# A pre-LN transformer block of 2048 tokens on one core: stored task places on all engines, a 64-row paired output projection, and transposes of two tiles at once

## The chip, the core and the metric

The kernel runs on one core of a Trainium2 chip. A core has TensorE (PE in the profile, with its weight loads as PEld), VectorE (DVE), ScalarE (ACT), GpSimd (POOL), and SyncE (SP), which here only issues DMAs. Each engine works through its own instruction queue in order and waits on semaphores. The metric is the device time of one execution in microseconds (us); lower is better.

## What is computed

x has 2048 rows of 448 in bf16, 16 heads of 28. The block is layer norm, linear attention with a Hedgehog feature map, a residual, layer norm, a gated unit of width 1792, a residual:

```
qkv = layernorm(x) @ wqkv                      # q, k, v of 16 heads x 28
pq, pk = q @ w_phi[h], k @ w_phi[h]
phi_q = concat(softmax(pq), softmax(-pq))      # phi_k likewise
kv = phi_k^T v ;  z = sum over tokens of phi_k # per head, over the whole sequence
o  = (phi_q kv) / (phi_q . z + 1e-6)
h  = x + o @ wo
g, u = layernorm(h) @ w_gate, layernorm(h) @ w_up
out = h + (sigmoid(g) * u) @ w_down
```

The sum over tokens in `kv` is a barrier: no token's `o` can begin before the last token's keys and values are in.

## The kernel before

The sequence is cut into 16 tiles of 128 rows. The program is a graph of tasks. Each task has an engine, a duration and a latency that the author wrote down, dependences, and where needed PSUM banks. `_Graph.order` lays the tasks out by a list scheduler, in Python, before anything runs: of the tasks that are ready it takes the one that can start first, and among those of an engine that could start within 0.05 us of each other the one with the largest rank. The rank is the length of the modelled work below the task, or a hand-set `bias`. What comes out is a fixed order per engine and a bank for each task; `emit` writes that order out with the semaphore waits. On the chip the order doesn't change, whatever the real durations are.

The stages, in the order in which a token passes them, by task name:

- `bst`, `agg`, `ve` (DVE), `rstd` (POOL, L449), `nm` (DVE, L452), `xn` (ACT, L461; DVE for the first two tiles): the first layer norm, in batches of 1, 1, 2, 4, 4 and 4 tiles. `xT` transposes the normed tile: by PE and an ACT copy (`xTp`, L469, L473) for four tiles, by a DMA transpose from SP (L477) of 128x512 for the other twelve.
- `wT`, `wTe`, `wM`, `W2` (L409 to L432) fold `w_phi` into the key and the query weights. `w_phi` is loaded by four DMAs of 6 KB straight into a zeroed block-diagonal tile. ACT empties all banks of the query fold and half of those of the key fold.
- `kp`, `vp` (PE, L484, L492), `ekp`, `ekm` (two exponentials, ACT), `v1` (ACT copy, L502), `ss`, `rs` (DVE), `phi` (POOL, L510), `kv` (PE, L519) for each tile.
- `q` (PE, L537) in 4 chunks of 512 tokens by 4 head groups, each followed by two exponentials on ACT (L547). `sigld` (L562) loads the sigmoid table on ACT, after all 32 of them.
- `kvz` (DVE) masks the finished `kv`; then per tile `num` (PE, L574, 8 matmuls of 120 columns, each into contiguous PSUM), `ocp` (ACT, L580), and on DVE `rSm`, `rr`, `b`, `c`, `rd`, `o`. `oT` transposes `o` (PE for 2 tiles, a DMA of 128x512 for 14, L620), `wo_` is the output projection of one tile (PE, L628, 4 matmuls of 112 rows), `h` the residual (DVE, L633).
- The second layer norm (`bst2` to `hn`, L664), its transpose `hT` (PE for 2 tiles, DMA for 14, L668), and the gated unit in chunks of 2, 4, 4, 4, 2 tiles: `gu` (L705, L707: 7 pairs of 64-row matmuls, the gate in array rows 0 to 63, the up projection in rows 64 to 127), `sig` (ACT, L714), `hh` (DVE, L722), `dn` (PE, L731, L741), `fin` (DVE, L747), `st` (SP, L749).

`f_warm` (L319) issues matmuls on the identity into a bank that the next PE task will own, where the plan sees PE idle.

```
order():  c = max((c for c in cands if c[0] <= emin + 0.05), key=lambda c: (c[1].rank, -c[1].idx))
wo_:      for g in range(G):
              r = e.matmul(bank[b][:, 0:D], lhsT=oT[:GP, t % 2, g, :], rhs=wo_sb[:, g, :],
                           start=(g == 0), stop=(g == G - 1))
num:      r = e.matmul(bank[bs[sg]][:, g * HL * E:(g + 1) * HL * E], ...
```

Of the kernel before, what the change touches and what calls it, by code (L numbers as in the profile page):

```python
# [5 lines left out]
dt = mybir.dt  # L6
# [4 lines left out]
P = 128  # L11
# [15 lines left out]

class _Task:
    __slots__ = ("name", "eng", "dur", "lat", "fn", "deps", "rank", "kind", "banks", "until", "got",
                 "start", "finish", "idx", "bias", "need", "lock", "hold", "warm")  # L30


class _Graph:
# [3 lines left out]
    PORT2 = ("xn", "rr", "b", "c", "o", "hn", "kvze")  # L37
    LAT = {"pe": 0.22, "act": 0.16, "dve": 0.08, "pool": 0.12, "sp": 0.0}
# [7 lines left out]
    def task(self, name, eng, dur, fn, deps=(), lat=None, bias=0.0, banks=None, until=(), kind=None):  # L46
# [4 lines left out]
        t.lat = self.LAT[eng] if lat is None else lat  # L51
# [4 lines left out]
        t.idx = len(self.tasks)  # L56
        t.need, t.hold, t.warm = list(t.deps), [], 0
# [9 lines left out]
    def order(self):  # L67
        tasks = self.tasks
        children = {n: [] for n in tasks}
# [16 lines left out]
        for n in reversed(topo):  # L86
            t = tasks[n]
            below = max((tasks[c].rank for c in children[n]), default=0.0)
            t.rank = max(below + t.dur + t.lat, t.bias)
# [4 lines left out]
        free = {e: 0.0 for e in self.ENGINES}  # L94
        bank_until = {}
# [19 lines left out]
        while True:  # L115
            best = None
            for e in self.ENGINES:
                cands = []
                for t in ready[e]:
                    est = max(free[e], port) if t.lock else free[e]  # L120
                    for d in t.deps:
                        est = max(est, tasks[d].finish)
                    pick = None
                    if t.banks is not None:
# [6 lines left out]
                        est = max(est, pick[0])  # L131
# [4 lines left out]
                c = max((c for c in cands if c[0] <= emin + 0.05), key=lambda c: (c[1].rank, -c[1].idx))  # L136
# [7 lines left out]
            t.finish = est + t.dur + t.lat  # L144
            if t.lock:
                port = est + t.dur
            if pick is not None:
                t.got = pick[1]
                for b in pick[1]:
                    t.hold += bank_until.get(b, [])  # L150
                    bank_until[b] = list(t.until)
# [9 lines left out]
        end = 0.0  # L161
        for t in done:
            if t.eng == "pe":
                if t.banks is not None and t.got is not None:
                    free_at = max([end] + [tasks[u].finish for u in t.hold] + [self.warm_from])
                    t.warm = max(0, int((t.start - free_at - 0.2) / 0.32))
                end = t.start + t.dur
        return done

    def emit(self, rings):  # L170
# [4 lines left out]
        with ExitStack() as es:  # L175
# [14 lines left out]
            for t in done:  # L190
                for ds in (t.hold, t.need):
# [5 lines left out]
                    if ds is t.hold and t.warm:  # L197
# [3 lines left out]
                        queues["pe"].append(lambda e, t=t: self.warm_fn(e, t.got[0], t.warm))  # L201
# [27 lines left out]
def build(nc, A_x, A_wqkv, A_w_phi, A_wo, B_w_gate, B_w_up, B_w_down, out):  # L229
# [15 lines left out]
    wo_v = A_wo.rearrange("(g hl d) n -> hl d g n", g=G, hl=HL)  # L245
    wd_v = B_w_down.rearrange("(ft p) n -> p ft n", p=P)

    NXD = 2
    NPE = 4
    NPT = 2  # L250
    NXP, NEK, NPHI, NV, NOP, NB2, NSG = 3, 3, 2, 3, 4, 2, 3

    with ExitStack() as es:
# [17 lines left out]
        xn_pad = sb("xn_pad", [P, NXP, KT, P])  # L271
        xnT = sb("xnT", [P, KT, S])
        wqkv_sb = sb("wqkv_sb", [GP, KT, 3 * D])
        Wq2 = sb("Wq2", [GP, KT, D])
        Wk2 = sb("Wk2", [GP, KT, D])
        Wphi = sb("Wphi", [GP, G, GP])
        wo_sb = sb("wo_sb", [GP, G, D])
# [9 lines left out]
        opm = sb("opm", [P, 2, 2, 2, G, E, HL])  # L287
        rSm = sb("rSm", [P, 2, 2 * G, HL], dt.float32)
        rr = sb("rr", [P, 2, 2 * G, HL])
        rden = sb("rden", [P, 2, 2 * G, HL])  # L290
        o_pad = sb("o_pad", [P, 2, 2 * G, P])
        oT = sb("oT", [P, 2, G, P])
# [22 lines left out]
        K = _Graph(nc)  # L315

# [3 lines left out]
        K.warm_fn, K.warm_deps, K.warm_from = f_warm, ["ident"], 1.2  # L320
# [8 lines left out]
        def TS(t):  # L329
            return slice(t * P, (t + 1) * P)  # L330


        task("z_phi", "pool", 0.45, lambda e: e.memset(Wphi[:], 0.0))
        task("ident0", "pool", 0.2, lambda e: e.memset(ident[:], 0.0))
        task("ident", "pool", 0.3, lambda e: e.affine_select(
            out=ident[:], in_=ident[:], compare_op=ALU.not_equal, fill=1.0, base=0, pattern=[[-1, P]],
            channel_multiplier=1), ["ident0"])
        task("z_xn", "pool", 0.3, lambda e: e.memset(xn_pad[:, :, :, GP:P], 0.0))
        task("neghalf", "pool", 0.1, lambda e: e.memset(neghalf[:], -0.5))
        task("v1one", "pool", 0.4, lambda e: e.memset(v1[:, :, :, DH:EV], 1.0))  # L340
# [7 lines left out]

# [9 lines left out]
        task("z_o", "pool", 0.3, lambda e: e.memset(o_pad[:, :, :, GP:P], 0.0))  # L358


        LD = 2.2

        def load(name, dst, src, eng="sp", deps=(), lat=LD, bias=0.0):
            task(name, eng, 0.5, lambda e: e.dma_start(dst, src), deps, lat=lat, kind="in", bias=bias)
# [3 lines left out]
        def load_x(t0, t1, **kw):  # L368
            load(("x", t0), x_sb[:, t0:t1, :], x_t[:, t0:t1, :], **kw)
            for t in range(t0, t1):  # L370
                x_ld[t] = ("x", t0)

        BIG = 1000.0
        load("wk", wqkv_sb[:, :, D:2 * D], wqkv_v[:, :, D:2 * D], bias=BIG, lat=3.4)
        load_x(0, 2, bias=BIG - 1, lat=3.8)
        load_x(2, 4, bias=BIG - 2, lat=4.2)
        load("wv", wqkv_sb[:, :, 2 * D:3 * D], wqkv_v[:, :, 2 * D:3 * D], bias=BIG - 3, lat=5.0)
        load_x(4, 8, bias=BIG - 4, lat=5.4)
# [413 lines left out]
```

## Time and profile before

| what | value |
|---|---|
| time, median of three runs | 233.93 us (233.16 to 235.45) |
| time of the profiled execution | 232.46 us |
| its span, first to last instruction | 230.7 us |
| mean granted TensorE clock | 0.993 |
| busy: PE, DVE, ACT, POOL | 212.6, 133.6, 120.8, 50.8 us |
| chain that ended last, by engine | PE 71%, ACT 11%, DVE 6%, DMA 6%, issue 3% |

Busy time is the union of the recorded instructions of an engine. Matmuls overlap in the pipeline and are recorded with their latency, so a PE that counts as busy can still be issuing at less than its rate; the distance from one start to the next says what a matmul costs in a stream. "Issue" in the chain is time in which an engine waited for nothing that the profile shows. The windows view gives the busy time of each engine in a chosen stretch.

### The profile page before, as it was taken

The page shows a single profiled execution, that of the slowest core. Times are in us where ns is not written, and L with a number is a line of the kernel's source. Part 1 is how long each engine was busy: PE and PEld are TensorE (multiplying, and loading weights), DVE is VectorE, ACT ScalarE, POOL GpSimd, SP SyncE. Part 2 cuts the span into 40 slices and gives each one's busy share as a digit, 9 for nine tenths or more (in the row PEclk, how much of TensorE's full clock was granted, in tenths as well). Part 3 has the DMA queues.
Part 4 walks back from the last instruction along what each step waited for, and adds up shares of the span by engine and source line. Part 5 has one row for each costly group of instructions (what it writes and reads, how often), then busy time and mean ns, then how long its engine had stood idle before and what let it go on. Part 6 is the DMA issues. An engine that isn't in the chain of part 4 may idle for free.

```text
span 230.7 us, 4738 instructions
## 1 busy us (share of the span) xinstructions
PE 212.6 (92%) x1845; PEld 115.3 (50%) x1845; DVE 133.6 (58%) x293; ACT 120.8 (52%) x213; POOL 50.8 (22%) x82
## 2 busy tenths in 40 slices
PE   6577979799989989899999999999999999999994
PEld 3343555466655656544444443444444444588542
DVE  1868889662389978778336666363366464245222
ACT  2498888878999767464424615342353322135000
POOL 4153579667000223041101020010000010100000
PEclk9997999999999999999999999999999999999999
DMA  6912555773543044723610223202002003210011
GB/s 186 295 50 66 139 134 142 159 195 77 146 133 48 0 88 64 117 54 64 126 39 3 40 25 83 60 3 60 20 3 45 3 1 80 67 35 3 21 40 40
DMA packets 37014, 17.04 MB, mean 74 GB/s; under 512 B 28416, under 2 KB 36096, under 8 KB 36992
## 3 DMA queue, kind: packets, MB, share of 16 engines
q1 hardware_dynamic: 36488, 16.72, 31.2%
q8 instruction: 14, 0.23, 0.4%
q10 hardware_dynamic: 504, 0.03, 0.2%
q14 instruction: 8, 0.07, 0.1%
HBM read 8.28 MB, written 1.84 MB: 44 GB/s over the span
## 4 chain that ended last, share of the span: by engine, by line
PE 71%; ACT 11%; DVE 6%; DMA 6%; issue 3%; POOL 1%; ACTq 0%; POOLq 0%; DVEq 0%
PE bank L705 34%; PE bank L731 17%; PE bank L628 4%; PE bank L484 4%; PE bank L537 3%; ACT opm L580 3%; ACT eq L547 3%; DMA Wphi<-in_A_w_phi_dram 2%; PE bank L492 2%; PE bank L519 2%; PE bank L741 2%; DMA oT<-o_pad 2%; ACT xn_pad L461 2%; DVE nm L452 1%; DMA xnT<-xn_pad 1%
## 5 line engine op out<-in xcount | busy, mean ns | idle before, releaser
L705 PE MATMUL bank<-hnT,wgu_sb 64*128 64x512 bf16 (+1 forms) x490 | 89.4, 334 | 1.3 <-DVE rs L638 0.8
L707 PE MATMUL bank<-hnT,wgu_sb 64*128 64x512 bf16 (+1 forms) x490 | 89.5, 334 | 0.0
L714 ACT ACTIVATE sg_sb<-bank 128x512 bf16<-128x512 f32 (+1 forms) x70 | 35.8, 511 | 65.1 <-PE bank L707 63.7
L705 PEld LDWEIGHTS bank<-hnT,wgu_sb 64*128 64x128 bf16 x490 | 44.0, 94 | 41.8 <-ACT sg_sb L714 4.2
L722 DVE TENSOR_TENSOR hh<-sg_sb,bank 128x512 bf16<-128x512 bf16 (+1 forms) x70 | 40.6, 580 | 41.1 <-ACT sg_sb L714 40.8
L707 PEld LDWEIGHTS bank<-hnT,wgu_sb 64*128 64x128 bf16 x490 | 44.0, 94 | 0.0
L731 PE MATMUL bank<-wd_sb,hh 128*128 128x448 bf16 x196 | 39.0, 353 | 0.2 <-DVE x_sb L747 0.2
L640 POOL TENSOR_TENSOR rs<-rs,neghalf 128x1 f32<-128x1 f32 x16 | 9.8, 610 | 122.3 <-DVE rs L638 122.3
L510 POOL TENSOR_TENSOR phi<-ek,rsum 128x896 bf16<-128x896 bf16 x16 | 27.0, 1697 | 12.4 <-DVE rsum L508 4.8
L731 PEld LDWEIGHTS bank<-wd_sb,hh 128*128 128x128 bf16 x196 | 18.4, 98 | 20.3 <-issue 2.3
L747 DVE TENSOR_TENSOR x_sb<-bank,x_sb 128x448 bf16<-128x448 f32 x16 | 10.0, 625 | 25.4 <-PE bank L731 21.6
L505 DVE TENSOR_REDUCE ssum<-ek 128x32 f32<-128x896 bf16 x16 | 17.1, 1076 | 9.3 <-ACT ek L499 9.2
L664 ACT ACTIVATE hn_pad<-x_sb,nm,rs 128x896 bf16<-128x896 bf16 x14 | 15.8, 1129 | 11.5 <-POOL nm L662 11.5
L547 ACT ACTIVATE eq<-bank 112x512 bf16<-112x512 f32 x32 | 17.1, 633 | 2.1 <-PE bank L537 1.9
L492 PE MATMUL bank<-wqkv_sb,xnT 112*128 112x448 bf16 x64 | 14.7, 357 | 2.8 <-ACT v L502 2.8
L484 PE MATMUL bank<-Wk,xnT 112*128 112x448 bf16 x64 | 15.9, 380 | 0.7 <-DMA xnT<-xn_pad 0.7
L537 PE MATMUL bank<-xnT,Wq 112*112 112x512 bf16 x64 | 15.6, 381 | 0.9 <-ACT eq L547 0.9
L580 ACT CAST opm<-bank 128x960 bf16<-128x960 f32 x16 | 15.5, 984 | 0.9 <-PE bank L574 0.9
L628 PE MATMUL bank<-wo_sb,oT 112*128 112x448 bf16 x64 | 14.8, 354 | 1.0 <-DMA oT<-o_pad 0.9
L444 DVE BATCH_NORM_STATS2 st<-x_sb 128x6 f32<-128x448 bf16 x16 | 9.3, 609 | 5.2 <-DMA x_sb<-in_A_x_dram 5.2
L461 ACT ACTIVATE xn_pad<-x_sb,nm,rs 128x448 bf16<-128x448 bf16 x14 | 10.1, 767 | 2.7 <-DVE nm L452 2.7
L633 DVE TENSOR_TENSOR x_sb<-bank,x_sb 128x448 bf16<-128x448 f32 x16 | 9.9, 622 | 2.1 <-PE bank L628 1.8
(75 smaller groups left out, 200.8 us busy)
## 6 DMA issues: line engine op xcount, KB each, us to landing
out_dram<-x_sb SPq DMA_DIRECT2D x16, 112.0 KB, 1.7
wgu_sb<-in_B_w_gate_dram SPq DMA_DIRECT2D x7, 224.0 KB, 3.8
wgu_sb<-in_B_w_up_dram SPq DMA_DIRECT2D x7, 224.0 KB, 4.1
wd_sb<-in_B_w_down_dram SPq DMA_DIRECT2D x7, 224.0 KB, 4.1
x_sb<-in_A_x_dram SPq DMA_DIRECT2D x3, 448.0 KB, 8.4
wqkv_sb<-in_A_wqkv_dram SPq DMA_DIRECT2D x3, 392.0 KB, 5.8
x_sb<-in_A_x_dram SPq DMA_DIRECT2D x2, 224.0 KB, 4.1
wo_sb<-in_A_wo_dram SPq DMA_DIRECT2D x4, 98.0 KB
```

What stands on the lines that cost most here:

```text
L484: r = e.matmul(bank[b][:, 0:D], lhsT=xnT[:GP, kt, TS(t)], rhs=Wk2[:, kt, :], start=(kt == 0), stop=(kt == KT - 1))
L492: r = e.matmul(bank[b][:, 0:D], lhsT=xnT[:GP, kt, TS(t)], rhs=wqkv_sb[:, kt, 2 * D:3 * D], start=(kt == 0), stop=(kt == KT - 1))
L510: task(("phi", t), "pool", 1.72, lambda e, t=t, s=s: e.tensor_tensor(phi[:, t % NPHI, :, :].rearrange("p a (h d) -> p (a h) d", d=DH), ek[ ...
L537: r = e.matmul(bank[b][:GP, :], lhsT=Wq2[:, kt, g * GP:(g + 1) * GP], rhs=xnT[:GP, kt, c * 512:(c + 1) * 512], start=(kt == 0), stop=(kt = ...
L547: task((key, g, c), "act", 0.5, lambda e, g=g, c=c, sg=sg, nm=nm: e.activation(eq[c][:, sg, g, :], bank[got(nm)[0]][:GP, :], ACT.Exp, scal ...
L580: task(("ocp", t), "act", 0.88, lambda e, t=t: e.copy(opm[:, (t // 2) % 2, :, t % 2, :, :, :].rearrange("p b g e h -> p b (g e h)"), pair[ ...
L628: r = e.matmul(bank[b][:, 0:D], lhsT=oT[:GP, t % 2, g, :], rhs=wo_sb[:, g, :], start=(g == 0), stop=(g == G - 1))
L705: e.matmul(bank[bg][:, 0:N], lhsT=wgu_sb[0:64, j, fs], rhs=hnT[0:64, j, cs], start=(j == 0), stop=(j == NJ - 1))
L707: r = e.matmul(bank[bu][:, 0:N], lhsT=wgu_sb[64:P, j, fs], rhs=hnT[64:P, j, cs], start=(j == 0), stop=(j == NJ - 1), tile_position=(64, 0))
L714: task(("sig", f_, c), "act", 0.5 if n == 4 else 0.3, lambda e, j=j, N=N, nm=nm: e.activation(sg_sb[:, j % NSG, 0:N], bank[got(nm)[0]][:, ...
L722: task(("hh", f_, c), "dve", 0.68 if n == 4 else 0.42, lambda e, j=j, N=N, nm=nm, f_=f_, c=c: e.tensor_tensor(hhT[c % 2][:, f_, 0:N], sg_s ...
L731: r = e.matmul(bank[b][:, 0:D], lhsT=hhT[c % 2][:, f_, ts], rhs=wd_sb[:, f_, :], start=(f_ == 0), stop=(f_ == FT - 1))
```

## The change

- **Order.** Every task gets a place from a table, `PLACE`, of some 950 whole numbers, by task kind in the order of creation; the rank of a task is minus its place. `order` still takes the earliest start first; the place decides among tasks of one engine within 0.05 us. The modelled durations are replaced (for instance `gu` 1.55 to 1.511, `hh` 0.68 to 0.605, `h` 0.62 to 0.545), hops between engines, a change between 64-row and full-row matmuls (`SWITCH` 0.098) and a DMA rate are added to the model.
- **Warm matmuls** now go into any bank that is free for the time (`plan_warm`), up to 110 us of the plan, instead of only into the bank of the waiting task.
- **Output projection.** `wo_sb` is laid out as 7 slices of 64 rows, held twice (partitions 0 to 63 and 64 to 127; 8 loads of 100 KB instead of 4). One `wo_` task takes two tiles: 7 pairs of 64-row matmuls, the first tile's in array rows 0 to 63 into one bank, the second's in rows 64 to 127 into another.
- **Transposes.** `xT` by DMA and `oT` by DMA take two tiles at once (7 and 7 instead of 12 and 14). PE transposes only 2 tiles of x instead of 4, and the first two tiles of `o` in one go. One small DMA transpose (`trw`) of the identity is added early.
- **num and o.** `num` writes its 120 columns as 30 runs of 4 fp32 at a stride of 16, so that heads lie innermost; `o` becomes one DVE instruction per tile.
- **Moves between engines.** Half of the query fold's copies and the `v1` copy of 4 tiles go from ACT to DVE; `nm` goes from DVE to POOL with its negation (`ng`) done ahead on DVE; `w_phi` comes by one DMA and is spread by a POOL multiply with the mask (`Wphi`).
- **Loads and batches.** x of tile 0 is loaded first; the loads of x beyond tile 1 come after `wq`. Layer-norm batches are 1, 1 and then 2 tiles. The query fold may use four banks.
- **Tail.** `dnp`, `fin` and `st` of the last two tiles are cut into column halves, `dn` may use two more banks.

```diff
+PLACE = {
+    "mask0": """-51""",
...
+    "q": """-58 -184 399 536 98 -50 14 144 172 167 -1593 -1608 -1566 -332 240 -2""",
...
+}
     def order(self):
...
+        for n, t in tasks.items():
+            if t.prio is not None:
+                t.rank = t.prio
...
+                    if e == "pe" and t.rows64 != rows64:
+                        est += self.SWITCH
                     for d in t.deps:
-                        est = max(est, tasks[d].finish)
+                        x = tasks[d]
+                        est = max(est, x.finish + self.HOP[e] if x.eng != e or e != "pe" else x.finish - 0.17)
...
+    def plan_warm(self, done):
+
+        held = {}
         for t in done:
...
+        end = self.warm_from
+        for t in done:
+            if t.eng != "pe":
+                continue
+            n = int((t.start - end - 0.3) / 0.32)
+            if n > 0 and t.start <= self.warm_to:
+                for b in range(7, -1, -1):
+                    past = [h for h in held.get(b, ()) if h[0] < t.start]
+                    if all(h[1] <= end for h in past):
+                        t.warm, t.warm_bank = n, b
+                        t.hold = list(past[-1][2]) if past else []
+                        break
+            end = max(end, t.start + t.dur)
...
-    NXD = 2
-    NPE = 4
+    XN_DVE = (0, 1)
+    NPE = 2
     NPT = 2
+    QLATE = 3
+    Q_FOLD, Q_EARLY = ("act", "dve"), True
+    XT_ENG = ("act",)
+    V_DVE = (3, 7, 11, 15)
+    BATCHES = [(0, 1), (1, 2), (2, 4), (4, 6), (6, 8), (8, 10), (10, 12), (12, 14), (14, 16)]
...
+        load("wphi", Wphi0[:], A_w_phi.rearrange("(g hl) i j -> (hl i) g j", hl=HL), 25, bias=BIG, eng="act")
+        task("Wphi", "pool", 1.0, lambda e: e.tensor_tensor(
+            Wphi[:].rearrange("p g (h d) -> p g h d", h=HL), Wphi0[:][:, :, None, :].to_broadcast([GP, G, HL, DH]),
+            maskK[:][:, None, :, None].to_broadcast([GP, G, HL, DH]), ALU.mult), ["wphi", "maskK"])
+        task("trw", "sp", 1.25, lambda e: e.dma_start_transpose(out=oT[:, 0, 0, :], in_=ident[:]), ["ident"],
+             lat=2.8, kind="tr")
...
-                task(("nm", a), "dve", 0.17, lambda e, a=a, z=z: e.scalar_tensor_tensor(
-                    nm1[:, a:z], mv1[:, a:z, 0], -1.0, rs1[:, a:z], op0=ALU.mult, op1=ALU.mult), [("rstd", a)])
+                task(("ng", a), "dve", 0.08, lambda e, a=a, z=z: e.tensor_scalar(
+                    nm1[:, a:z], mv1[:, a:z, 0], -1.0, None, op0=ALU.mult), [("agg", t) for t in range(a, z)])
+                task(("nm", a), "pool", 0.2, lambda e, a=a, z=z: e.tensor_tensor(
+                    nm1[:, a:z], nm1[:, a:z], rs1[:, a:z], ALU.mult), [("ng", a), ("rstd", a)])
...
+            elif t % 2 == 0:
+                task(("xT", t), "sp", 1.25, lambda e, t=t: e.dma_start_transpose(
+                    out=xnT[:, t // 2, :, :, :].rearrange("p a k s -> p (a k) s"),
+                    in_=xn_pad[:, (t // 2) % NXP, :, :, :].rearrange("p a k s -> p (a k s)")),
+                    [("xn", t), ("xn", t + 1)], lat=1.78, kind="tr")
...
-                        r = e.matmul(bank[bs[sg]][:, g * HL * E:(g + 1) * HL * E],
+                        r = e.matmul(bank[bs[sg]][:, 0:E * H].rearrange("p (e h) -> p e h", h=H)[:, :, g * HL:(g + 1) * HL],
                                      lhsT=eq[c][:, sg, g, (t % 4) * P:(t % 4 + 1) * P], rhs=kvz[:, sg, g, :, :],
                                      start=True, stop=True)
...
+                for j in range(NJ):
+                    e.matmul(bank[b[0]][:, 0:D], lhsT=oT[0:64, tb, j, :], rhs=wo_sb[0:64, j, :],
+                             start=(j == 0), stop=(j == NJ - 1))
+                    r = e.matmul(bank[b[1]][:, 0:D], lhsT=oT[64:P, tb, j, :], rhs=wo_sb[64:P, j, :],
+                                 start=(j == 0), stop=(j == NJ - 1), tile_position=(64, 0))
...
+            task(("wo_", t), "pe", 1.33, f, [("oT", t)] + [("wo", a, d) for a in range(2) for d in range(4)],
+                 banks=WO_BANKS, until=[("h", t), ("h", t + 1)], rows64=True)
```

## The prediction

> **What bounds the kernel now.** I read the page's slices and chain first: PE 71% of the chain, but 92% busy, which by itself would leave 18 us. So I cut the span into stages at the places where the PE timeline changes character and asked the windows view for each engine's busy time there. Columns: stage, its length, then busy us (and instructions) of PE, PEld, DVE, ACT, POOL, the granted clock, the DMA share, GB/s.
>
> ```profile
> core 0: us, PE busy (x) PEld busy (x) DVE busy (x) ACT busy (x) POOL busy (x), PEclk, DMA share, GB/s
> 0.00:8.45 8.45, 5.58 (x29) 2.85 (x29) 3.29 (x11) 2.25 (x3) 3.58 (x18) 1.00 0.82 221
> 8.45:20.00 11.55, 7.11 (x73) 5.08 (x74) 8.74 (x26) 9.39 (x19) 4.45 (x5) 0.99 0.43 117
> 20.00:50.00 30.00, 26.46 (x204) 16.15 (x203) 23.07 (x43) 25.74 (x53) 19.81 (x14) 0.95 0.58 139
> 50.00:59.90 9.90, 9.90 (x74) 6.44 (x73) 3.89 (x7) 7.92 (x16) 6.50 (x4) 1.00 0.39 96
> 59.90:79.35 19.45, 17.99 (x163) 10.99 (x162) 14.91 (x44) 18.27 (x31) 2.09 (x5) 1.00 0.38 97
> 79.35:98.70 19.35, 16.91 (x236) 11.85 (x238) 15.61 (x44) 12.61 (x23) 3.73 (x9) 1.00 0.50 83
> 98.70:218.90 120.20, 120.20 (x1035) 58.12 (x1032) 61.55 (x122) 44.61 (x71) 10.66 (x30) 1.00 0.18 40
> ```
>
> The kernel is two kernels. From 98.70, where the second `gu` chunk starts, PE never lacks work until the tail. Before that ACT is the fullest engine: 61.3 of the 70.9 us from 8.45 to 79.35, the start of the first `gu`; what PE does there comes late because ACT, or a latency in front of ACT, is late. The waits of ACT between 8 and 80 us (who waited, for whom, total, times, longest) and three steps of the chain (start, length, what) say which:
>
> ```profile
> ACT xn_pad L461 <- DVE nm L452: 2.7, 2, 1.6
> ACT Wk L432 <- PE bank L424: 2.3, 1, 2.3
> ACT v L502 <- PE bank L492: 2.0, 2, 1.2
> ACT eq L547 <- PE bank L537: 1.9, 2, 1.2
> ```
>
> ```profile
> 26.13 1.01 issue
> 27.14 1.02 POOL rs L449
> 28.19 1.66 DVE nm L452
> ```
>
> The largest is the layer-norm batch of four: after the POOL power, `nm`, which takes 0.16 us at other times, lasts 1.65 us while POOL runs `phi` beside it, twice, and ACT stands.
>
> How much PE loses I get from the PE timeline by start-to-start distances, not by busy time: a `kp` or `vp` 0.755 us, a `q` 0.865, a `kv` or `num` 0.42, a `wo_` 0.76, a half-size `gu` 0.765, a fold group of four 0.22. The work done before 98.70 is then 16 x 2 x 0.755 + 16 x 0.865 + 16 x 0.42 + 12 x 0.42 + 8 x 0.76 + 14 x 0.765 + 16 x 0.22 + 2.5 for the other transposes = 72.5 us. PE's first useful matmul starts at 4.95. So 93.75 - 72.5 = 21 us of PE are unused before 98.70, 1.2 of them at changes of row mode, whose price these rows of the timeline show (start, length, instruction):
>
> ```profile
> 121.06 0.38 PE L707 MATMUL bank<-hnT,wgu_sb 64*128 64x512 bf16 x1
> 121.27 0.38 PE L705 MATMUL bank<-hnT,wgu_sb 64*128 64x512 bf16 x1
> 121.27 0.38 PE L707 MATMUL bank<-hnT,wgu_sb 64*128 64x512 bf16 x1
> 121.58 0.93 PE L628 MATMUL bank<-wo_sb,oT 112*128 112x448 bf16 x4
> 122.44 0.39 PE L705 MATMUL bank<-hnT,wgu_sb 64*128 64x512 bf16 x1
> ```
>
> A pair of 512 columns takes 0.215, so the `wo_` could have started at 121.485 and started 0.10 later; four matmuls take 0.76, and the next pair came 0.10 later still. Each change costs 0.10.
>
> **The change part by part**, against the profiled execution: 232.46 us, span 230.7, so 1.8 around it. The median of the runs is 1.5 above that execution.
>
> *The front, up to the first `gu` (79.35).* The bound is ACT. It idles 70.9 - 61.3 = 9.6 us there. The change takes from it four fold copies (0.43 from start to start in the ACT timeline), four `v1` (0.42) and two `xT` copies (0.49): 1.7 + 1.7 + 1.0 = 4.4 us. If ACT were packed the stage would end 14.0 us earlier. The edits that aim at the idle time: batches of two instead of four and `nm` on POOL (nearest row: POOL's 0.19 us product of mean and rstd in the second layer norm, L660) remove both 1.65 us waits and shorten what precedes them; a query fold done early makes `q` available as PE work, and `eq` as ACT work, in the gaps where neither has anything now (its last copy ends at 48.6, first `q` at 51.6). What keeps it below 14: kv sums remain a barrier, POOL still has 16 x 1.70 = 27.2 us of `phi` plus some 7 us, and each tile must pass ACT, DVE, POOL and PE in turn. Ends: 0 (all idle time reappears elsewhere) to 14.0. I take 70%, 9.8 us, because PE and DVE allow it: PE's work to that point is 72.5 - 10.7 - 4.3 = 57.5 us in 64.6, DVE's 54 in 64 of the new length, with some 5 us of `v1` and fold copies added and 3.6 us of `nm` taken away.
>
> *`Wphi`, load order, `trw`.* The first fold matmul waits for the last of four small loads, 5.5 us after issue, at 8.45. One load instead, plus a POOL multiply of 448 columns: the nearest row, `phi` with 896 columns, is 1.70, so 0.85 to 1.7. Against it the one load stands where the first of the four is issued, 1.29 against 2.78, 1.5 us sooner. Net -0.7 to +1.7, I take +0.5. `trw` (1.2 us of SP, as the other transposes) stands in SP's empty stretch from 6 to 17.8 us: nothing is queued behind it that is due. If SP has x loads behind it, it costs those 1.2 us, covered by DVE's backlog of statistics. x of tile 0 in front of `wk` is 112 KB at about 290 GB/s, 0.4 us later for the key transposes, hidden behind the `Wphi` wait.
>
> *From first `gu` to PE saturation (19.35 us).* Useful work is 10.7 + 4 x 0.76 + 3 x 0.42 = 15.0, so 4.3 are lost, 1.2 to mode changes, the rest to waits for `rstd`, `oT` (0.9) and `opm`. `wo_` in 64-row form next to `gu` costs no change. Two tiles per transposition: the 128x896 transposes land after 2.9 us against 2.5 for 128x512, so a pair costs 0.4 more latency for its first tile and 2.1 less than two in a row. Ends 0 to 3.5; I take 1.5.
>
> *PE work in the saturated part.* A pair of 448 columns, scaled from the 0.215 row, takes 0.189; seven are 1.32 us for two tiles against 1.51. Four such pairs fall after 98.70: 0.8. Five of the eight `wo_` there now stand between two `gu`: ten changes at 0.10, 1.0. Together 1.8 (0.8 if they come to stand beside `dn`, where they add changes). A pair holds two banks until both `h` are done instead of one; `gu` has three bank pairs of its own, and `h` is 0.54 from start to start, so nobody waits. `o` as two DVE instructions of 448 columns costs 2 x 0.29 against 0.54 (DVE timeline), 7 x 0.04, beside 60 us of free DVE time.
>
> *`num` into strided PSUM.* No row of this trace has a matmul with a gapped destination. The floor is the present 0.42 per tile. From above, the recorded latency of one such matmul, 0.217, unpipelined: 128 x (0.217 - 0.053) = +21 us of PE. I take 0, since each run of 4 fp32 is written whole and the same 120 values leave; the top end is a rival. The Trainium skill speaks against this edit: "PSUM — Partial Sum Buffer", section Specifications (TRN2), gives cache lines of 8 bytes and says "any non-contiguous AP slows matmuls significantly", without a factor. No row here shows it. Were the factor two, the sum below would be 6.7 us worse, an estimate from that sentence.
>
> *Tail.* The last `fin` is 0.62 and its store 1.7; halves make that 0.31 and a little less: 0.5. Beyond it the same 5.3 us of `dn` per two tiles remain.
>
> Sum: -9.8 + 0.5 - 1.5 - 1.8 - 0.5 = -13.1. 232.46 - 13.1 = 219.4; against the median, 220.8. I say 220.
>
> **The rivals.**
>
> 1. *The gaps close further.* Front 14.0, all 3.5 of the next stage, the rest as above: 232.46 - 14.0 - 3.5 - 1.8 - 0.5 = 212.7, 214 on the median. For it: none of PE, DVE, POOL is full in the front. Against: ACT would have no wait in 57 us.
>
> 2. *The order does little.* The places choose only among tasks within 0.05 us; the order stays greedy, and waits move rather than go. Then only moved work and content count: 2 us of the front, 1.8, 0.5, less 0.5: 228.7, 230 on the median. For it: ACT's waits of 8.45 to 79.35 are many and small (the largest group is 2.7 us). Against: `nm` and the late query fold are causes with a name, and both go.
>
> 3. *Slower: `num` pays for its stride.* At the top price, +21 us of PE: 219.4 + 21 = 240.4, 242 on the median. It decides from 128 x 0.102 us, that is when a `num` matmul takes 0.155 instead of 0.053. For it: nothing in this profile is like it. Against: the same 16-byte pieces per partition, and half of the `num` (those before `gu`) may hide behind ACT.
>
> 4. *An engine gets stuck behind a wait*, as an in-order queue with a fixed order can when a transposition or load lands late: 227 to 234.
>
> **How the numbers follow.** Chances: forecast (216 to 226) 0.58, rival 1 (209 to 216) 0.17, rival 2 (226 to 233) 0.14, rival 3 0.06, rival 4 or another loss 0.05. Leaving out the far ends of rivals 1 and 2 and rival 3, 212 to 229 holds 8 in 10. 1% is 2.3 us, about what a measurement here can tell from no change: faster than 231.6 are the first two and most of rival 2, 0.87; within, 0.05; slower 0.08.
>
> **What would show it.** First `gu` near 70 us instead of 79.35 and second chunk near 88; ACT over 90% busy between 9 and 70; no `nm` row over 0.3 us; `wo_` pairs at 0.19 from start to start, with no 0.10 around them beside `gu`; `num` still 0.42 per tile. It is wrong if ACT's idle time before the first `gu` stays near 9 us, if `num` stretches, or if PE waits appear after the second chunk.

## The result and the profile after

| | before | after |
|---|---|---|
| time, median | 234.33 us (233.16 to 235.45, 4 runs) | 220.74 us (220.06 to 221.35, 4 runs) |
| profiled execution | 232.46 us, span 230.7 | 221.35 us, span 219.6 |
| PE busy in the span | 212.6 us | 206.8 us |
| first `gu` starts | 79.35 us | 75.63 us |
| recorded end of the last matmul | 227.65 us | 216.37 us |

The kernel became faster: ratio 0.942 of the time before, 95% interval 0.9364 to 0.9476. The profiled pair differs by 11.1 us, less than the medians (13.6), since the profiled execution of before was below its median and that of after above it. The sums below go by the profiled pair. Runs over 1.5% above the fastest of their kernel count as slow and are left out of the ratios but not of the medians: two of the four of experiment 3, and of experiment 5 the one that was profiled.

The windows view of the changed kernel, cut where the stages change (stage, length, busy us and instructions of PE, PEld, DVE, ACT, POOL, granted clock, DMA share, GB/s):

```profile
core 0: us, PE busy (x) PEld busy (x) DVE busy (x) ACT busy (x) POOL busy (x), PEclk, DMA share, GB/s
0.00:5.77 5.77, 3.60 (x8) 1.04 (x8) 1.58 (x6) 1.28 (x1) 2.96 (x15) 1.00 0.63 179
5.77:20.00 14.23, 12.53 (x106) 8.81 (x107) 11.91 (x37) 11.67 (x23) 3.74 (x8) 0.88 0.78 178
20.00:50.00 30.00, 26.71 (x200) 15.97 (x199) 23.24 (x48) 26.19 (x55) 25.14 (x21) 1.00 1.06 181
50.00:58.50 8.50, 8.50 (x72) 5.50 (x70) 4.73 (x8) 5.86 (x12) 5.05 (x3) 1.00 0.01 2
58.50:75.60 17.10, 15.32 (x168) 9.31 (x166) 15.02 (x45) 15.70 (x25) 1.49 (x2) 1.00 0.48 122
75.60:100.40 24.80, 24.20 (x317) 17.17 (x317) 23.16 (x71) 15.71 (x25) 8.88 (x24) 1.00 0.38 72
100.40:216.40 116.00, 115.97 (x1052) 61.50 (x1050) 53.36 (x103) 40.04 (x66) 5.27 (x18) 1.00 0.19 38
```

Look at the row 20.00:50.00. PE does 26.71 us of it, hardly more than before (26.46), though ACT, POOL and DVE are not full either, and the DMA share has risen from 0.58 to 1.06. In the next row, which takes in the last `kv` (it ends at 56.65, counted here and below as the start of its last matmul plus 0.05), PE is full: the transpositions are all in by then.

What PE waits for up to 110 us (line, for whom, total, times, longest), and two pieces of the chain of waits between 20 and 60:

```profile
PE bank L648 <- DMA xnT<-xn_pad: 3.3, 4, 1.4
PE bank L555 <- DMA wqkv_sb<-in_A_wqkv_dram: 2.1, 2, 1.7
PE bank L462 <- POOL ident L485: 1.8, 1, 1.8
PE bank L743 <- ACT opm L749: 0.9, 3, 0.5
PE bank L801 <- DMA oT<-o_pad: 0.3, 1, 0.3
...
```

```profile
31.24 6.89 DMA xnT<-xn_pad
...
42.19 6.79 DMA xnT<-xn_pad
```

The chain no longer goes over the layer norm's `nm`; it goes twice through a DMA transposition of a pair of x tiles, for 6.89 and 6.79 us. The third line is a wait of the warm matmuls for the identity at the start. From issue to landing (last number) the transpositions take

```profile
hnT<-hn_pad SPq DMA_TRANSPOSE x14, 2.9
...
xnT<-xn_pad SPq DMA_TRANSPOSE x7, 6.3
oT<-o_pad SPq DMA_TRANSPOSE x7, 3.0
```

6.3 us in the median for x (3.3 to 7.2), where the smaller ones of before took 2.5 (2.4 to 4.0). The 896 columns of `hnT` and `oT`, about as large, take 2.9 and 3.0. The trace also has when each transfer lands: those that SP issues land in the order of issue, without exception in this trace and in the twelve others. The pair issued at 42.19 lands at 48.98, 0.85 after the weight load issued ahead of it (41.02, lands at 48.13).

A part of the front belongs to this execution and not to the kernel. From 9.61 to 13.03 its granted clock was 0.50:

```profile
9.61:13.03 3.42, 3.37 (x29) 2.65 (x27) 3.38 (x11) 3.03 (x7) 0.54 (x1) 0.50 1.14 199
```

The first `vp` matmuls there start up to 0.37 apart, later ones 0.19. (The profile of before has such a stretch too, from 19.79 to 23.20.) Experiment 9 below has the same order and the same instructions up to `num`; in its profile the query weights land at 7.24 instead of 8.60, no such stretch occurs, the last `kv` ends at 54.56 and the first `gu` starts at 73.56, 2.1 sooner. Both marks are given below where a front is compared.

**Where the 11.1 us came from.** I laid out PE's blocks by start-to-start distances once more, and call unused what is neither a useful matmul nor its own pipelined issue: waits, warm matmuls, and changes between 64-row and full-row matmuls (row mode, below).

| stage | before | after | gain |
|---|---|---|---|
| first useful matmul to 20 us | 6.5 (from 4.95) | 3.3 (from 5.77) | 3.2 |
| 20 to 50 | 7.2 | 4.8 | 2.4 |
| 50 to the first `gu` | 3.3 | 4.8 | -1.5 |
| first `gu` to second chunk | 4.4 | 2.3 | 2.1 |
| second chunk to the last `dn` stretch | 4.0 | 0.7 | 3.3 |
| last stretch | 0.8 | 0.2 | 0.6 |
| sum | 26.2 | 16.1 | 10.1 |
| useful matmul time | 196.5 | 194.5 | 2.0 |

Against these 12.1 us stand 0.8 for the later first matmul and 0.15 for the part after the last one: 11.1.

In the saturated part the change is visible at once. Rows of the PE timeline around an output projection (start, duration, line):

```profile
113.60 0.38 PE L882 MATMUL bank<-hnT,wgu_sb 64*128 64x512 bf16 x1
113.60 0.38 PE L884 MATMUL bank<-hnT,wgu_sb 64*128 64x512 bf16 x1
113.82 0.35 PE L801 MATMUL bank<-wo_sb,oT 64*128 64x448 bf16 x1
113.82 0.35 PE L803 MATMUL bank<-wo_sb,oT 64*128 64x448 bf16 x1
114.00 0.35 PE L801 MATMUL bank<-wo_sb,oT 64*128 64x448 bf16 x1
...
114.95 0.35 PE L803 MATMUL bank<-wo_sb,oT 64*128 64x448 bf16 x1
115.14 0.38 PE L882 MATMUL bank<-hnT,wgu_sb 64*128 64x512 bf16 x1
```

`wo_` begins 0.22 after the last `gu` pair and the next `gu` 0.19 after the last `wo_` pair: seven pairs in 1.32 us, two tiles, with no 0.10 on either side. The blocks of `gu` and of `dn` have also become long runs: after the second chunk the row mode changes 5 times instead of 35.

### The profile page after: what moved, and what is told of

The parts are those of the page before. It is cut to its first block, busy times and chain, and to the rows that moved or that the text cites. A ratio compares the mean times of both kernels' runs of the same rounds, so it can differ in the third digit from the quotient of the medians.

```text
span 219.6 us, 4860 instructions
## 1 busy us (share of the span) xinstructions
PE 206.8 (94%) x1912; PEld 119.3 (54%) x1912; DVE 133.4 (61%) x315; ACT 116.5 (53%) x203; POOL 52.5 (24%) x91
## 4 chain that ended last, share of the span: by engine, by line
PE 67%; ACT 12%; DMA 10%; DVE 6%; issue 2%; SPq 1%; POOL 0%
PE bank L882 36%; PE bank L908 17%; DMA xnT<-xn_pad 6%; PE bank L801 4%; ACT eq L715 3%; DMA wqkv_sb<-in_A_wqkv_dram 3%; ACT xn_pad L612 2%; PE bank L918 2%; ACT ek L661 2%; PE bank L704 2%; ACT opm L749 2%; PE bank L656 2%; ACT v L669 1%; ACT ek L663 1%; DMA oT<-o_pad 1%
## 5 line engine op out<-in xcount | busy, mean ns | idle before, releaser
L882 PE MATMUL bank<-hnT,wgu_sb 64*128 64x512 bf16 (+1 forms) x490 | 87.2, 333 | 0.5 <-DVE st L812 0.3
L884 PE MATMUL bank<-hnT,wgu_sb 64*128 64x512 bf16 (+1 forms) x490 | 87.2, 334 | 0.0
L882 PEld LDWEIGHTS bank<-hnT,wgu_sb 64*128 64x128 bf16 x490 | 45.4, 94 | 38.5 <-issue 1.2
L884 PEld LDWEIGHTS bank<-hnT,wgu_sb 64*128 64x128 bf16 x490 | 45.3, 94 | 0.0
L908 PE MATMUL bank<-wd_sb,hh 128*128 128x448 bf16 x196 | 37.6, 353 | 0.2 <-DVE hh L899 0.2
L908 PEld LDWEIGHTS bank<-wd_sb,hh 128*128 128x128 bf16 x196 | 18.9, 98 | 18.7 <-issue 0.8
L929 DVE TENSOR_TENSOR x_sb<-bank,x_sb 128x448 bf16<-128x448 f32 (+1 forms) x18 | 10.2, 572 | 22.7 <-PE bank L908 19.0
L817 POOL TENSOR_TENSOR rs<-rs,neghalf 128x1 f32<-128x1 f32 x16 | 10.1, 634 | 53.0 <-DVE rs L815 52.9
L715 ACT ACTIVATE eq<-bank 112x512 bf16<-112x512 f32 x32 | 18.6, 647 | 1.9 <-PE bank L704 1.9
L648 PE MATMUL bank<-Wk,xnT 112*128 112x448 bf16 x64 | 14.6, 353 | 3.3 <-DMA xnT<-xn_pad 3.3
L704 PE MATMUL bank<-xnT,Wq 112*112 112x512 bf16 x64 | 16.4, 381 | 0.1
L801 PE MATMUL bank<-wo_sb,oT 64*128 64x448 bf16 x56 | 11.9, 349 | 0.4 <-DMA oT<-o_pad 0.3
L803 PE MATMUL bank<-wo_sb,oT 64*128 64x448 bf16 x56 | 11.9, 350 | 0.0
```

Of the source, the lines that this page charges most:

```text
L704: r = e.matmul(bank[b][:GP, :], lhsT=Wq2[:, kt, g * GP:(g + 1) * GP], rhs=xnT[:GP, 2 * c:2 * c + 2, :, kt, :], start=(kt == 0), stop=(kt = ...
L715: task((key, g, c), "act", 0.48, lambda e, g=g, c=c, sg=sg, nm=nm: e.activation(eq[c][:, sg, g, :], bank[got(nm)[0]][:GP, :], ACT.Exp, sca ...
L801: e.matmul(bank[b[0]][:, 0:D], lhsT=oT[0:64, tb, j, :], rhs=wo_sb[0:64, j, :], start=(j == 0), stop=(j == NJ - 1))
L882: e.matmul(bank[bg][:, 0:N], lhsT=wgu_sb[0:64, j, fs], rhs=hnT[0:64, j, cs], start=(j == 0), stop=(j == NJ - 1))
L884: r = e.matmul(bank[bu][:, 0:N], lhsT=wgu_sb[64:P, j, fs], rhs=hnT[64:P, j, cs], start=(j == 0), stop=(j == NJ - 1), tile_position=(64, 0))
L908: r = e.matmul(bank[b][:, 0:D], lhsT=hhT[c % 2][:, f_, ts], rhs=wd_sb[:, f_, :], start=(f_ == 0), stop=(f_ == FT - 1))
```

## The experiments

Theory at the start: the stored places close the gaps in the front, by about 10 us. Rival: the order does little, moved work and content count (the prediction's second rival). Experiments 2 to 11 hold the changed kernel's order fixed on every engine, written out as a table (`ORDER`), so that an edit does not reshuffle the plan; experiment 9 (220.23 us) shows that writing it out costs nothing that can be measured. The ratios are to runs of the kernel before that were taken with each experiment.

**1. Without the table.** The rank falls back to the modelled length of the work below.

```diff
-            t.prio = -PLACE[key][made[key]]
+            t.prio = None
```

> The changed kernel without the stored places: the rank is the modelled work below a task, as before the change, with the new durations and every other edit. Theory, the table carries the gain: PE's unused time fell by 10 us and the rows at which PE changes row mode fell from some 35 to 10 after the second gu chunk began, both of which only an order can do, so the time goes from 220.7 to 226 to 230 us. Rival, the fitted durations and the new content carry it: 219 to 222.5 us.

230.88 us (230.11 to 231.46), just above the theory's range, ratio 0.9891 (0.9857 to 0.9925). The table holds 10 of the 13.6 us; everything else alone is worth 1.1%. The rival is refuted. The first `gu` comes at 81.67, 6.0 later than with the table; PE's unused time before it is some 5 us more. One part of the expectation falls: the row mode changes 22 times in this kernel and 20 with the table (48 before). The long runs therefore come not from the table but from the rest of the model; that its price for a change (`SWITCH`) does it is the likely reason, and was not tried by itself.

**2. Weight loads behind the x transpositions.** The 22 loads of `wo`, `w_gate` and `w_up` move on SP's queue behind the last `xT`.

SP's part of `ORDER`, in outline:

```diff
 xT(2)
-wo, wg, wu loads (22) between xT(2) and xT(14)
 xT(14)
+wo (8), wg and wu (14) loads
```

> The changed kernel with its order written out and kept on every engine, but the 22 loads of wo, w_gate and w_up (4 MB) stand on SP behind the last x transposition instead of between them. Theory: the two-tile x transposes land after 6.3 us because these loads fill the DMA engines from 20 to 49 us, and PE stands some 4 us before kp for them; then they land in 3 to 3.5 us and the time falls by 2 to 4 us, to 217 to 219. Rival a, ACT or POOL takes over as the bound: 219.5 to 221. Rival b, the weights come too late for wo_ and gu: 222 or more.

224.31 us (223.61 to 224.55), ratio 0.9624 (0.9573 to 0.9674): slower than the changed kernel, but the front did what the theory says. The transpositions land after 3.2 us, the last `kv` ends at 50.47 instead of 56.65 (54.56 in experiment 9), and PE is full from 20 to 50. Windows view of this kernel, and PE's largest wait:

```profile
20.00:50.00 30.00, 30.00 (x242) 18.94 (x241) 24.54 (x46) 27.71 (x58) 28.61 (x24) 1.00 0.49 89
50.00:58.50 8.50, 8.16 (x78) 5.56 (x78) 5.62 (x19) 8.10 (x15) 0.00 (x0) 1.00 1.04 218
58.50:75.60 17.10, 10.61 (x91) 5.65 (x90) 9.79 (x27) 8.51 (x15) 1.49 (x2) 0.70 0.74 159
```

```profile
PE bank L1766 <- DMA oT<-o_pad: 7.3, 2, 6.3
```

The gain was given back in the next stage: now the transposition of `o` stands behind the loads (it lands at 69.55, the last load at 68.78), PE waits 6.3 us for it at one stroke, and the granted clock of that stage is 0.70. The first `gu` comes at 77.45.

**3. Two transpositions of one x tile instead of a pair**, with the loads where the changed kernel has them.

The lines are shortened:

```diff
-  out=xnT[:, t // 2, :, :, :], in_=xn_pad[:, (t // 2) % NXP, :, :, :]      # 128x1024
+  out=xnT[:, t // 2, t % 2, :, :], in_=xn_pad[:, (t // 2) % NXP, t % 2, :, :]   # 128x512, twice
```

> The changed kernel with its order written out and kept, but each pair of x tiles is transposed by two DMAs of 128x512, one behind the other at the place of the one of 128x1024, and kp and vp wait for their own tile. Theory, the loads in front of a transposition make it late: landing stays at 5 us or more, time 220 to 222. Rival, the size of the two-tile transposition makes it late: landing near 2.5 us as before the change, PE's 4 us before kp go, 217 to 219.

224.27 us, above both ranges expected, with a wide spread (220.49 to 226.59) that allows no ratio. The trace is clearer: the small ones land after 5.5 us in the median, PE waits 4.2 us for them, the last `kv` ends at 58.6. Size is not what makes them late.

**4. `nm` back on DVE**, without `ng` (in outline).

```diff
-  ng (dve): nm1 = -mean;  nm (pool): nm1 = nm1 * rs1
+  nm (dve): nm1 = (mean * -1.0) * rs1
```

> The changed kernel with its order written out and kept, but nm is again one DVE instruction behind the POOL power, without the negation ahead of it; batches stay at two tiles. Theory, DVE beside POOL's phi made nm last 1.65 us: some of the seven rows last over 0.5 us and the time rises by 1 to 3 us, 221.7 to 224. Rival, the batch of four was the cause and the engine of nm is indifferent: all rows near 0.16 us, 220 to 221.5.

221.60 us (220.72 to 222.87), ratio 0.9516 (0.9455 to 0.9578): 0.9 us above the changed kernel, within the intervals. The mechanism shows in the trace: two of the seven `nm` on DVE fall beside a `phi` on POOL and are stretched, where the others take 0.10 to 0.15 us. Timeline of DVE in this kernel:

```profile
26.66 0.84 DVE L1556 SCALAR_TENSOR_TENSOR nm<-mv,rs 128x2 f32<-128x2 f32 x1
30.47 1.06 DVE L1556 SCALAR_TENSOR_TENSOR nm<-mv,rs 128x2 f32<-128x2 f32 x1
```

The `phi` beside the second one:

```profile
29.82 1.70 POOL L1633 TENSOR_TENSOR phi<-ek,rsum 128x896 bf16<-128x896 bf16 x1
```

It ends at 31.52, the `nm` at 31.53; both of the kernel before end in the same way, 0.02 us after the `phi` in which they start. On POOL all seven `nm` take 0.19. The stretch has not gone from the changed kernel, though. Its negation `ng`, which stayed on DVE, meets a `phi` once and lasts until 0.03 us after that `phi`'s end:

```profile
29.09 1.22 DVE L598 TENSOR_SCALAR nm<-mv 128x2 f32<-128x2 f32 x1
```

**5. Also `w_down` later.** As experiment 2, and the 7 loads of `w_down` behind the transposition of tiles 4 and 5 of `o`.

SP's part of `ORDER` beyond experiment 2, in outline:

```diff
-wd loads (7) in front of oT(2)
+oT(2), oT(4), wd loads (7)
```

> The changed kernel with its order written out and kept, the 22 loads of wo, w_gate and w_up behind the last x transposition on SP as in the run before, and in addition the 7 loads of w_down behind the second DMA transposition of o instead of in front of the first. Theory: with the loads out of the way the last kv ended at 50.5 instead of 57.1, and the gain was given back only where the first oT waited 6.3 us behind the loads; w_down is not needed before 90 us, so now oT lands in 3 us and the kernel keeps some 5 us: 214 to 217. Rival: the 3.9 MB of the other loads alone last until oT, 219 to 223.

218.25 us (216.79 to 220.27), ratio 0.9306 (0.9229 to 0.9382). The `oT` land after 3.1 us in the median, the last `kv` ends at 52.05, the first `gu` comes at 73.60. By the medians it is 2.5 us better than the changed kernel, though above the 214 to 217 expected: from 52 to 73.6 PE has some 7 us unused, 1.5 of it in a wait for the first `oT`, and the granted clock is 0.50 from 66.46 to 69.87. That first `oT`, which this stage waits for, still stands behind loads, those of `w_gate` and `w_up`: it is issued at 62.23 and lands at 66.34, 0.76 after the last of them (65.58). The rival's cause is thus present in this kernel, though its time did not come. The rest of the stage passes through `num`, its copy on ACT, six DVE steps, `wo_` and the second layer norm.

**6. `wo_` in two passes**: the seven matmuls of the upper rows after the seven of the lower rows.

```diff
                 for j in range(NJ):
                     e.matmul(bank[b[0]], lhsT=oT[0:64, ...], rhs=wo_sb[0:64, j, :], ...)
+                for j in range(NJ):
                     r = e.matmul(bank[b[1]], lhsT=oT[64:P, ...], rhs=wo_sb[64:P, j, :], ...)
```

> The changed kernel with its order written out and kept, but a wo_ task issues its seven matmuls of array rows 0 to 63 first and then the seven of rows 64 to 127, so that the two row halves can't run side by side. Same work, same banks. Theory, PE is the bound from the first gu on: each wo_ takes 2.65 instead of 1.33 us, six of the eight stand behind the first gu, 8 us, and some of the two before it: 228 to 231. Rival, PE has slack there: 221 to 224. If the halves never ran side by side: 220 to 221.5.

223.51 us (223.33 to 223.68), ratio 0.9551 (0.9504 to 0.9599): 2.8 us, not 8 to 10. The halves overlapped all the same. PE timeline of this kernel (L1766 the lower rows, all seven first in the program; L1769 the upper rows; L1848 the lower rows of the next `gu`; x2 marks two matmuls in one row):

```profile
115.70 0.54 PE L1766 MATMUL bank<-wo_sb,oT 64*128 64x448 bf16 x2
115.91 0.35 PE L1769 MATMUL bank<-wo_sb,oT 64*128 64x448 bf16 x1
116.08 0.35 PE L1766 MATMUL bank<-wo_sb,oT 64*128 64x448 bf16 x1
...
116.65 0.38 PE L1848 MATMUL bank<-hnT,wgu_sb 64*128 64x512 bf16 x1
116.67 0.54 PE L1769 MATMUL bank<-wo_sb,oT 64*128 64x448 bf16 x2
```

An upper-row matmul starts at 115.91, while lower-row ones that stand ahead of it in kernel.py start at 116.08 and after. (So on PE the order of the program is not in every case the order on the chip. Whether the compiler or the chip changed it, the traces don't tell.) Each half keeps to its own order, and the upper half falls 0.57 to 0.59 us behind the lower. That lag is paid when full-row matmuls follow: the two `wo_` in front of the first `gu` take 2.00 us from their start to the next `num`, where paired ones take 1.43. Inside a run of 64-row matmuls it is not paid again: from the sixth `wo_` (107.96) to the eighth (119.67) it is 11.71 us here, as in the changed kernel (106.45 to 118.16). Two before the first `gu`, three behind it and once for the last three make 6 x 0.57 = 3.4 us; the time rose by 2.8. That PE sets the end there is borne out; how much pairing is worth is less than its busy time says.

**7. No warm matmuls.** The number of warm matmuls in front of a task, the third field of `ORDER`, is 0 everywhere (five rows, 13 matmuls; one row is shown).

```diff
-[["wT", 1, 0], [0], 8, 7, []],
+[["wT", 1, 0], [0], 0, 7, []],
```

> The changed kernel with its order written out and kept, without any of the 13 matmuls on the identity that fill PE's idle time. Theory, they hold the granted clock: without them the fold and the first kp run at a lower clock, as at 19.8 to 22.7 us before the change, and the time rises by 1 to 4 us, 221.7 to 225. Rival, PE has slack in the front and the clock there costs nothing: 220 to 221.5.

222.45 us (221.16 to 223.69), ratio 0.9505 (0.9443 to 0.9568): 1.7 us, in the range expected, although the intervals overlap. The trace shows the cause that the theory named: the first `vp` matmuls, from 12.69 on, start 0.37 and 0.36 apart and from 13.4 on 0.19, where in experiment 9, with the warm matmuls, they are 0.19 apart from 10.33 on. (The clock column of the windows view reads 1.00 over this stretch, so the starts are the better witness.) The warm matmuls are no guarantee, as the half-clock stretch in the changed kernel's own profile shows. And `wk` lands at 6.79 in this profile instead of 5.73, so part of the difference may be a late load.

**8. ACT gets work back**: all copies of the query fold and `v1` of four tiles.

```diff
-    Q_FOLD, Q_EARLY = ("act", "dve"), True
-    V_DVE = (3, 7, 11, 15)
+    Q_FOLD, Q_EARLY = ("act",), True
+    V_DVE = ()
```

> The changed kernel with its order written out and kept, but the four copies of the query fold and the four v1 copies that DVE took over are on ACT again, at the same places in the order: 3.4 us of ACT before the first gu. Theory of the prediction, ACT is the bound of the front: the time rises by 2 to 3.5 us, 222.7 to 224.2. Rival, the front is bound by the late x transpositions and ACT has slack: at most 1 us more, 220 to 221.7.

221.65 us (220.74 to 222.48), ratio 0.9471 (0.9416 to 0.9525). ACT does 3.0 us more between 8.45 and the first `gu`, and that `gu` comes at 74.95, against 75.63 in the changed kernel and 73.56 in experiment 9, whose profile is like this one in its clock (1.00). ACT's busy time there in four kernels, by the windows view: changed, experiment 9, experiment 8, experiment 10.

```profile
8.45:75.63 67.18, 61.84 (x523) 38.55 (x524) 53.56 (x131) 57.76 (x109) 34.19 (x32) 0.97 0.72 138
```

```profile
8.45:73.56 65.11, 59.86 (x512) 36.88 (x512) 52.57 (x129) 57.27 (x109) 33.92 (x31) 1.00 0.71 141
```

```profile
8.45:74.95 66.50, 59.88 (x517) 36.86 (x515) 49.71 (x123) 60.77 (x117) 33.88 (x31) 1.00 0.71 139
```

```profile
8.45:70.55 62.10, 59.11 (x511) 36.64 (x512) 52.66 (x130) 57.03 (x109) 33.71 (x31) 1.00 0.62 123
```

The changed kernel leaves ACT 67.18 - 57.76 = 9.4 us idle, experiment 9 7.8. Experiment 8, with some 3 us more work, leaves 5.7; its `gu` starts 1.4 us later than in experiment 9, and its time is 0.9 to 1.4 us longer than those of the two kernels by the medians, with intervals that overlap. That is at most half of the added work, and within the rival's range. Experiment 10 leaves 5.1 with ACT's work untouched, by an earlier `gu`. ACT had slack, and something else held the front; that its work was wholly free is not shown.

**9. `num` without the stride.** The 120 columns go to one run of PSUM again, and all behind `num` is left as it is, so that it reads the values with heads and columns exchanged.

```diff
-  bank[bs[sg]][:, 0:E * H].rearrange("p (e h) -> p e h", h=H)[:, :, g * HL:(g + 1) * HL]
+  bank[bs[sg]][:, g * HL * E:(g + 1) * HL * E]
```

> The order of the changed kernel, written out; the num matmuls write their 120 columns in one run of PSUM again, nothing else is altered, so that ocp and all behind it read the values with heads and columns exchanged (the output differs). Theory (the gapped destination costs nothing: 0.42 to 0.43 us per tile in the changed kernel as in the kernel before): 0.42 per tile again, 220 to 222 us. Rival (the stride costs something that the modelled ends hide): num under 0.40 per tile and 1 to 3 us less, 218 to 220.

220.23 us (219.81 to 221.49), ratio 0.9453 (0.9348 to 0.9558): the same as the changed kernel. A `num` takes 0.42 to 0.43 per tile from start to start in both. The groups' lines (busy us, mean ns), changed kernel and this one:

```profile
L743 PE MATMUL bank<-kvz,eq 112*128 112x120 bf16 x128 | 9.3, 217 | 0.9 <-ACT opm L749 0.9
```

```profile
L1708 PE MATMUL bank<-kvz,eq 112*128 112x120 bf16 x128 | 9.3, 217 | 0.9 <-ACT opm L1714 0.9
```

**10. Without `trw`**, the small transposition of the identity; loads as in experiment 5.

```diff
-        task("trw", "sp", 1.25, lambda e: e.dma_start_transpose(out=oT[:, 0, 0, :], in_=ident[:]), ["ident"],
-             lat=2.8, kind="tr")
```

> The kernel with late loads of weights and of wd (218.25 us), without the small transpose trw of the identity. Theory (trw takes a first-time cost upon itself: it took 2.04 us to issue and landed after 7.9 in the changed kernel, the x pairs with late loads land after 3.2): the first x pair takes its place, lands after 6 us or more, the first kp of tile 2 comes 2 to 4 us later, and 1 to 3 us are lost: 219 to 221. Rival (trw only stands in SP's queue): the first x pair lands after 3 to 4 us, its issue comes no later, 217 to 218.5.

218.13 us (217.05 to 219.48), ratio 0.9348 (0.9247 to 0.9449). No first-time cost passes to the x pairs, as the rival said: they land after 3.1 us in the median and 4.5 at most, and the first is issued at 9.34 instead of 10.32. The first `gu` comes at 70.55 in the profile. The median is that of experiment 5, so what `trw` costs or saves is below what these runs can tell; the profile of experiment 5 has two stretches at half clock and this one none. The first `oT` again lands 0.77 after the last load of `w_up` (64.92 and 64.15). With experiment 5 this is the fastest version, about 2.5 us below the changed kernel by the medians; the intervals of the ratios still overlap (0.9306 and 0.9348 against 0.942).

**11. Single x transpositions with the loads late.** Experiment 3's edit in the kernel of experiment 5.

> The kernel with late loads of weights and of wd (218.25 us), with each x pair transposed by two DMAs of 128x512 instead of one of 128x1024. With the loads early this made the landing 5.5 us. Theory (the loads made the transposes late, not their size): each lands after 2.4 to 3 us, the time is 217.5 to 219.5. Rival (the pair is what costs: its first tile waits for both): kp of every even tile comes 0.5 us sooner and the last kv ends 1 to 2 us sooner, 216 to 217.5. Should two DMAs cost SP more than they save, 219.5 to 222.

219.70 us (218.87 to 220.06), ratio 0.9407 (0.9326 to 0.9489). They land after 2.5 us, as in the kernel before: with the loads out of the way one tile costs 2.5 and a pair 3.2. The last `kv` ends at 50.33 in the profile, 1.7 earlier than in experiment 5, but the first `gu` hardly moves (73.26): PE waits 3.1 us for the first `oT` instead of 1.5. That `oT` is issued 1.7 us earlier (60.51) and lands at 66.16, where it landed at 66.34 before: again 0.77 after the last load of `w_up` (65.39). The time is just above the theory's range and well above the rival's: an earlier barrier was worth nothing, because the transposition behind it waited for the same loads.

## Why the prediction was right, and where it was not

The time was forecast as 220 and came as 220.74. The direction, the case (gaps close, then PE) and the total hold, but two terms missed in opposite directions, and that the total came so near is in part luck. The forecast sum was -13.1 on the profiled execution; that pair shows -11.1, the medians -13.6.

- **Front, -9.8: mis-sized, -3.7 measured** for the first `gu` (this takes in the `Wphi` term). The step that failed is "The bound is ACT." The moved work did leave it: ACT is busy 57.76 instead of 61.33 us before the first `gu`, 3.6 of the 4.4 counted. But its idle time stayed at 9.4, against 9.6, and that was the sign by which the prediction said it would be wrong. First `gu` near 70 and ACT over 90% busy did not come (75.63 and 86%; 73.56 and 88% in experiment 9). Of the 5.6 us that are missing against the 70 forecast, 2.1 belong to the half clock and the late weights of the one execution, since experiment 9 does not have them. Some 3 were lost to the x transpositions, for which the prediction had no term (its "2.9" is for pairs of `o`): with the weight loads issued among them they took 6.3, and with the loads out of the way the first `gu` came at 70.55 (experiment 10, also without `trw`, at full clock like experiment 9). Experiments 2, 5 and 11 show it from one side (loads moved: 3.2 for pairs, 2.5 for singles, last `kv` 4.1 to 4.6 us earlier than in a profile with a like clock), experiment 3 from the other (smaller transpositions, loads kept: 5.5), and experiment 8 shows that ACT had slack. The prediction counted the transposition's own latency and not what its queue carries ahead of it.
- **The cause named for the gaps, `nm`, was right as a mechanism.** No `nm` row is over 0.3 (all 0.19 on POOL), and back on DVE it is stretched to 0.84 and 1.06. Its worth was small and not settled: 0.9 us. The negation left on DVE is itself stretched once, to 1.22.
- **`Wphi`, +0.5.** PE's first useful matmul came 0.8 later. The multiply itself was done at 4.9, well before the 8.45 at which the fold began in the kernel before; what held the fold, which starts at 9.30, was the arrival of the weights. `wk` landed at 5.73, and then the transposes of the query weights, which stand ahead of the fold on PE, waited 1.7 us for `wq` (landed at 8.60). The stored places decide the order of the loads, and they put x of tiles 2 and 3 first, `wk` second and x of tile 0 third, other than the description of the change above has it.
- **First `gu` to second chunk, -1.5: right**, -2.1 of unused time. The stage itself became longer, 24.8 us, since it now holds two `dn`, `wo_` for six tiles instead of four, and six `num` instead of three.
- **Saturated part, -1.8: undersized.** The price of a mode change was right and was paid far less often: 30 changes fewer behind the second chunk at 0.10 are 3.0 of the 3.3 us. The prediction counted only the ten beside `wo_`, and not that `gu` and `dn` would be laid in long runs. The pairs cost 1.32 against a forecast 1.32; six after the first `gu` at 0.18 to 0.19 saved make 1.1.
- **`num`, 0: right.** The stride costs nothing that can be measured (experiment 9). "PSUM — Partial Sum Buffer", section Specifications (TRN2), in the Trainium skill says that any access that isn't contiguous slows matmuls significantly; for a destination in runs of 16 bytes these traces show 217 ns and 0.42 per tile both ways, and the measurement decides.
- **Tail, -0.5: right**, 0.6 less unused and 0.15 more after the last matmul.
- **The rivals.** That the order does little was refuted by experiment 1. That `num` pays was refuted by the trace and experiment 9. That the gaps close further was not reached by the change, but experiments 5 and 10 go part of the way. A queue stuck behind a late landing came true in small, at the transpositions, and cost a few us inside the forecast's range rather than the 227 to 234 given for it.

What stays open: how much each of the parts other than the table is worth alone (together 1.1%), and whether a plan made anew with the later loads would shorten the chain behind the barrier. The late loads were only tried by hand in the fixed order, and no run has the first `oT` free of loads with the x transpositions free of them too. Nor was a transposition issued from another queue than the loads.

## What to carry to other kernels

Before crediting an engine's idle time to a better order, ask what ends each wait, and for a DMA transposition ask what loads are in front of it on its queue in the new order: here moving the weight loads behind the transpositions was worth about 2.5 us by the medians, with intervals that overlap. Loads moved out of one stage's way stand in the way of the next latency-critical transfer, so move them past that too (experiment 2 against 5; in 5, 10 and 11 the first `oT` still waits). Count changes of row mode over the whole plan and not only at the instruction that is edited.

## What the runs showed of the hardware

- Transfers issued by SP land in the order of issue in all thirteen traces. A DMA transposition behind queued loads lands after 6.3 us instead of 3.2 (128x1024) and 5.5 instead of 2.5 (128x512); the one of the small identity, issued right behind the first loads, after 6.2 to 8.4.
- Matmuls in the upper 64 rows of the array start ahead of lower-row ones that stand before them in kernel.py (115.91 against 116.08, experiment 6); within a half the order stays, and the lag of one half (0.57 to 0.59) is paid only when full-row matmuls follow. "TensorE: Matmul & The Clock Gate" in the Trainium skill, Part 3, says of matmuls "strict FIFO, no reordering". These rows show otherwise for 64-row halves, unless the compiler had already changed the order.
- `nm` and `ng`, DVE instructions on one to four values per partition, take 0.10 to 0.17 us alone; every one that starts during a `phi` on POOL ends 0.02 to 0.03 after that `phi`, in all thirteen traces (0.41 to 1.65 long).
- When PE waited 6.3 us for one transposition, the granted clock of that stage fell to 0.70 (experiment 2), against 1.00 in the changed kernel's same stage.
